# Super-step 0 of a delta-rule attention kernel in another order, with unused products in TensorE's waits

## The chip, the cores and the metric

The kernel runs on one core of one Trainium2 chip. The metric is device time in microseconds (us), from one launch to its end; smaller is better.

The engines are named as in the profile: PE is TensorE (matmul) and PEld its weight loads, DVE is VectorE, ACT is ScalarE, POOL is GpSimd, SP is SyncE, which here only issues DMAs. Each engine has a queue of its own and works it off in order; engines wait for each other through semaphores. TensorE writes to PSUM alone; ScalarE and VectorE copy from there to SBUF.

## The reference

Three layers follow each other. The first is a delta rule over 768 steps, for 4 batches of 8 heads of 48 dimensions; the other two are dense, on 3072 tokens.

```python
k_n = k / (np.linalg.norm(k, axis=-1, keepdims=True) + 1e-06)
for t in range(S):
    kt, vt, bt = (k_n[:, :, t], v[:, :, t], beta[:, :, t, None])
    y[:, :, t] = np.einsum('bhd,bhde->bhe', q[:, :, t], state)
    v_old = np.einsum('bhde,bhd->bhe', state, kt)
    state = state + bt[:, :, :, None] * np.einsum('bhd,bhe->bhde', kt, vt - v_old)
x = y.transpose(0, 2, 1, 3).reshape(B * S, H * D)        # 3072 x 384
h = np.maximum(x @ w_in, 0.0)                            # 384 -> 2048
x = h * h @ w_out                                        # 2048 -> 384
g = x @ w_gate                                           # 384 -> 1536
out = (g * (1.0 / (1.0 + np.exp(-g))) * (x @ w_val)) @ w_out2
```

## The kernel before, in words

**Super-steps.** The sequence is cut into six super-steps J of 128 steps, each into two chunks c of 64, and the 32 pairs of batch and head into two halves p of 16. Within a chunk the recurrence is solved in closed form: G = K K^T of the chunk, masked to its strict triangle and scaled by beta and the key norms, gives a matrix whose inverse (of 1 minus it) is needed. Then U = inverse times (V minus keys times state), Y = masked (K Q^T) times U plus the state's part, and the state gains K^T U. The dense layer 1 follows for the tokens of a super-step, in 16 slices m of 128 hidden features; layer 2 follows at the end for all.

**What stands at the start.** Super-steps 1 to 5 run their attention in the shadow of the dense layers of the step before. Super-step 0 has nothing to hide behind, so its order is written out by hand (lines 1154 to 1269), and for every engine alone: the manual schedule makes each engine's queue follow the order of the program's text. The line that calls a stage is `run(("name", ...))`; what a stage does is in the functions of the same name:
- `gram0` (line 437): G of a chunk on TensorE, into PSUM. `gd` (450) copies its four 32x32 diagonal blocks to DG, half p=0 on ScalarE, half p=1 on VectorE; `go` (461) copies an off-diagonal block, negated, to NT on ScalarE, two copies a call.
- `din` (499): VectorE transposes DG into T (a matrix per partition), copies the diagonal out (the squared norms), ScalarE takes their root, VectorE multiplies T by the mask BM (line 504), refines the root (`root`, line 377, eight operations on 32 columns) and multiplies T by beta (506).
- `inv0` (624): the inverse of the 16x16 blocks in T, on VectorE. `dout` and `nrows` transpose back, into ND and NDT. `d1` and `d2` (669, 687) merge 16x16 blocks to 32x32 on TensorE; `t11` transposes on VectorE; `dcopy` (521) copies the diagonal blocks from ND to NT, two copies on ScalarE and two on VectorE; `m1` and `m2` (710, 723) merge to 64x64, and their results are copied by ScalarE (p=0) and VectorE (p=1).
- `u` (753): U on TensorE, scaled by beta on VectorE (764). `y` (814, line 829): Y on TensorE, copied to x0, the input of the dense layer. `ku` (774) is the state's gain.
- `amm`, `acopy`, `asel`: K Q^T of a chunk on TensorE, copied by ScalarE, masked by GpSimd (595).
- `mcopy`, `mmask`, `mbeta`, `mout`, `tload`: G of super-step 1, copied by ScalarE, masked by GpSimd (482), scaled by VectorE (486), stored to DRAM by SP's queue (549) and read back as T, in which GpSimd runs the long inverse `inv` (600) of super-step 1.

**Conversion of weights.** The weights of layer 1 come in pieces (pc, kd) of 256 features, kd=0 of w_in and kd=1 of w_out, each as 64-bit words, and are turned into 32-bit floats: first an Abs on ScalarE (line 157, at `begin`), then three steps on VectorE (162, 164, 169). `conv(n)` does n of the steps, `ahead()` and `far(n)` begin the next piece or the next n. The Abs writes a buffer f, of which there is one while `held` is set, and two that alternate (by `turn`) afterwards. Slice m of the dense layer needs piece (m//2, 0) for its first product (line 952) and (m//2, 1) for its second (1031).

**The planner.** From line 1281 on, the dense slices of super-step 0 run with stages put between them at due times (`first`, in units of slices); a `slot` runs what is due and then as many conversion steps as a rate allows.

**Buffers.** PSUM has three buffers of tag "a", two of "h", three of "t". At the start half p=0 of most products goes to "a" and half p=1 to "t".

Of the kernel before, what the change touches and what calls it, by code (L numbers as in the profile page):

```python
# [8 lines left out]
F32 = mybir.dt.float32  # L9
# [3 lines left out]
ALU = mybir.AluOpType  # L13
# [8 lines left out]
def delta_attention_moe_moe2_kernel(  # L22
# [37 lines left out]
    nc = tc.nc  # L60
# [20 lines left out]
    ps_a = ctx.enter_context(tc.tile_pool(name="ps_a", bufs=3, space=bass.MemoryType.PSUM))  # L81
    ps_h = ctx.enter_context(tc.tile_pool(name="ps_h", bufs=2, space=bass.MemoryType.PSUM))
# [7 lines left out]
    ap = att.__enter__()  # L90
# [17 lines left out]
    ND, NDT, DG, BM = (t[:, 0:1024].rearrange("p (x t) -> p x t", t=32) for t in (own_w, own_v, own_h, own_l))  # L108
    ident = own_l[:, 1024:1152]
    TD = [t[:, 1024:1536].rearrange("p (u h t) -> p u h t", u=2, h=8) for t in (own_w, own_v)]  # L110
    KB = {}
    T = ap.tile([128, 32, 32], F32, name="T")
# [25 lines left out]
    turn = [0]  # L138
    held = [1]

    class Piece:
# [18 lines left out]
        def run(self):  # L160
            f, fi = self.f, self.f.bitcast(I32)
            nc.vector.tensor_scalar(out=fi, in0=fi, scalar1=3, scalar2=None, op0=ALU.logical_shift_left)  # L162
            yield
            nc.vector.scalar_tensor_tensor(  # L164
                out=self.d[:, 1], in0=self.d[:, 1], scalar=-0x80000000, in1=fi,
                op0=ALU.bitwise_and, op1=ALU.bitwise_or,
            )
            yield
            nc.vector.scalar_tensor_tensor(  # L169
                out=self.d[:, 1], in0=self.d[:, 0], scalar=29, in1=self.d[:, 1],  # L170
                op0=ALU.logical_shift_right, op1=ALU.bitwise_or,
            )
            yield
# [42 lines left out]
    begun = {}  # L216
# [3 lines left out]
    def load_w1(pc, kd, eng=nc.sync):  # L220
        if (pc, kd) == FIRST:
            raw = xp.tile([128, 2 * PIECE], I32, tag="xh", name="raw")
        else:
            raw = wp.tile([128, 2 * PIECE], I32, tag="w", name="raw")
        load_piece((w_in, w_out)[kd], pc, kd == 1, raw, eng)
        loaded[pc, kd] = raw
        landing[pc, kd] = 0 if startup else clock[0] + LAND + (eng is nc.sync)
# [24 lines left out]
    def ahead():  # L252

        if conv1 and landed(conv1[0]):
            begin(conv1[0])

    def far(n):

        for job in conv1[0:n]:
            if landed(job):  # L260
                begin(job)

    def landed(job):

        return job in loaded and clock[0] >= landing[job]
# [54 lines left out]
    startup = [True]  # L320
# [178 lines left out]
    def d_in():  # L499

        nc.vector.transpose(out=T, in_=DG.rearrange("s x t -> s t x"))
        nc.vector.tensor_copy(SS_, T.rearrange("p a b -> p (a b)")[:, 0:1024:33])
        nc.scalar.activation(out=A_, in_=SS_, func=ACTF.Sqrt)
        nc.vector.tensor_tensor(T, T, BM, op=ALU.mult)
        root(SS_, A_, B_, NT_, bT)
        nc.vector.tensor_tensor(T, T, bT.unsqueeze(1).to_broadcast([128, 32, 32]), op=ALU.mult)

# [302 lines left out]
    x0 = []  # L810
# [3 lines left out]
    def y0(c, p):  # L814

        if c == 0:
            pys = [
                (ps_t if g else ps_a).tile([128, KD, 64], F32, tag="t" if g else "a", name="ps_y") for g in range(2)
            ]
            rows = [slice(64 * g, 64 * g + 64) for g in range(2)]  # L820
        else:
            py = bank(p, [128, KD, 2, 64], "ps_y")
            pys = [py[:, :, g] for g in range(2)]
            rows = [slice(0, 112), slice(0, 128)]

        def product(quarter, g, h, w0, start, stop):

            q0, r = 32 * (quarter % 4), rows[g]
            nc.tensor.matmul(
                pys[g][q0:q0 + 32, quarter // 4], RSF[p][r, g, 64 * h + w0:64 * h + w0 + 32], AQ[c][r, p, g, h],  # L830
                start=start, stop=stop,
            )

        for i in range(4):
            for g in range(2):
                product(3 * i, g, 2 * i, 0, True, True)
                product(3 * i + 1, g, 2 * i, 32, True, False)
                product(3 * i + 2, g, 2 * i + 1, 16, True, True)
                product(3 * i + 1, g, 2 * i + 1, -16, False, True)
        if not x0:  # L840
            x0.append(xp.tile([128, KD, TOK], F32, tag="xl", name="x0"))
        t0 = c * HT + p * 128
        for y, t1, n in [(pys[0], t0, 64), (pys[1], t0 + 64, 64)] if c == 0 else [
            (py.rearrange("q k g t -> q k (g t)"), t0, 128)
        ]:
            ts = slice(t1, t1 + n)
            (copy2 if startup and t1 % 128 else copy)(x0[0][:, :, ts], y)

    def fetch_x(J, c0, n_):
        xr = ap.tile([128, KD, HT], F32, tag="xf", bufs=2, name="xr")  # L850
# [294 lines left out]
    def run_all(names):  # L1145
        for n in names:
            run(n)
# [3 lines left out]
            load_w1(pc, 0), load_w1(pc, 1)  # L1151


    pad = ap.tile([32, 16], F32, name="pad")
    nc.vector.memset(pad, 0.0)
    lead = ps_h.tile([128, 8, 64], F32, tag="h", name="ps_lead")
    for _ in range(15):
        nc.tensor.matmul(lead[0:16, 0, 0:16], pad, pad, start=True, stop=True)
    nc.vector.memset(TMP[:, 0:1], 1.0)
    nc.scalar.activation(out=TMP[:, 1:2], in_=TMP[:, 0:1], func=ACTF.Sqrt)  # L1160
    order = ctx.enter_context(ExitStack())
    order.enter_context(
        tc.manual_schedule(engines={mybir.EngineType.DVE, mybir.EngineType.Pool, mybir.EngineType.Activation})
    )

    def conv(n):

        conv_to(converted() + n)

    P2 = range(2)  # L1170
    mark = ap.tile([128, 1], F32, name="mark")

    def stage(w, J, c):
        run_all((w, J, c, p) for p in P2)

    def merge16(w, c):
        run_all((w, c, p) for p in P2)
# [19 lines left out]
    run(("v", 0, 0))  # L1197
    run(("v", 0, 1))
    load_w1(1, 0)
    nc.gpsimd.memset(mask, 0.0)  # L1200
    for b0 in (0, 64):
        nc.gpsimd.affine_select(
# [6 lines left out]
    run(("brows",))  # L1209
    for c in P2:  # L1210
        run_all(("gd", c, p) for p in P2)
    run(("din",))
    run_all(("go", c, p) for c in P2 for p in P2)
    run_all(("gram0", 1, c) for c in P2)
    run(("sums", 1, 0))
    run_all(("amm", 0, c) for c in P2)
    stage("mcopy", 1, 0)
    run(("sq", 1, 1, 0))
    stage("mcopy", 1, 1)
# [17 lines left out]
    ahead()  # L1237
    merge16("d2", 0)
    run(("t11", 0, 0))
    conv(1)  # L1240
    load_w1(0, 1, nc.scalar)
    run(("m1", 0, 0))
    run(("dcopy", 0))
    load_w1(1, 1, nc.scalar)
    load_w1(2, 0, nc.scalar)
    nc.gpsimd.tensor_copy(mark, NT[0][1][:, 0, 0:1])
    run(("m2", 0, 0))
    conv(2)
    load_w1(2, 1, nc.scalar)
    run(("asel", 0))  # L1250
    run(("asel", 1))
    run(("u", 0, 0))
    stage("mbeta", 1, 0)
    stage("mout", 1, 0)
    run(("y", 0, 0, 0))
    ahead()
    run(("y", 0, 0, 1))
    stage("mbeta", 1, 1)
    stage("mout", 1, 1)
    conv(3)  # L1260
    ahead()
    held.clear()
    run(("tload", 1, 0))
    run(("tload", 1, 1))
    run(("v", 1, 0))
# [15 lines left out]
    if True:  # L1281
# [7 lines left out]
        for J in range(NJ):  # L1289
            seq += [(J, c0, HT, m) for c0 in (0, HT) for m in range(HMS[J])]  # L1290
            seq += [(J, 0, TOK, m) for m in range(HMS[J], NM1)]
        first = {
            0: [("d1", 1, 0), ("d1", 1, 1), ("abs", 2), ("ku", 0, 0)],
            0.5: [("abs", 2), ("d2", 1, 0), ("d2", 1, 1), ("loadw", 3, 0, nc.scalar)],
            1: [("ks", 0, 1), ("t11", 0, 1), ("dcopy", 1), ("loadw", 3, 1, nc.scalar)],
            1.5: [("loadw", 4, 0, nc.scalar)],
            2: [("m1", 0, 1), ("loadw", 4, 1, nc.scalar)],
# [55 lines left out]

        moe1_h(*seq[0])
        moe1_low()
        far(1 + len(begun))
        for n, it in enumerate(seq):
            J, c0, n_, m = it
            if n and J and not seq[n - 1][0]:
# [111 lines left out]
```

## Time and profile before

| | us |
|---|---|
| median of 3 runs | 1034.11 (1033.69 to 1034.76) |
| time of the profiled execution | 1035.7 |
| span of the profiled execution | 1034.0 |
| PE busy | 995.0 |
| DVE busy | 588.2 |
| ACT busy | 401.2 |
| POOL busy | 251.2 |

The span is the time from the program's first instruction to its last, in one profiled execution. A row of the profile tells of a group of instructions: the line of the kernel, the engine, the operation, what it writes and reads (out<-in, by the program's names), partitions x elements, and how many (x). In a timeline the first two numbers are the start and the time in us from the first instruction's start to the last's end; in brackets stands the idle time of the engine before it, and what ended it. "issue" is time for which the profile shows nothing that was waited for. POOL's times are rough, and matmuls overlap in their pipeline, so that the mean of a run of them is the time of the run over their count.

### The profile page before, as it was taken

The page shows a single profiled execution, that of the slowest core. Times are in us where ns is not written, and L with a number is a line of the kernel's source. Part 1 is how long each engine was busy: PE and PEld are TensorE (multiplying, and loading weights), DVE is VectorE, ACT ScalarE, POOL GpSimd, SP SyncE. Part 2 cuts the span into 40 slices and gives each one's busy share as a digit, 9 for nine tenths or more (in the row PEclk, how much of TensorE's full clock was granted, in tenths as well). Part 3 has the DMA queues.
Part 4 walks back from the last instruction along what each step waited for, and adds up shares of the span by engine and source line. Part 5 has one row for each costly group of instructions (what it writes and reads, how often), then busy time and mean ns, then how long its engine had stood idle before and what let it go on. Part 6 is the DMA issues. An engine that isn't in the chain of part 4 may idle for free.

```text
span 1034.0 us, 24233 instructions
## 1 busy us (share of the span) xinstructions
PE 995.0 (96%) x10508; PEld 813.4 (79%) x10508; DVE 588.2 (57%) x951; ACT 401.2 (39%) x752; POOL 251.2 (24%) x368
## 2 busy tenths in 40 slices
PE   5688999999999999999999999999999999999998
PEld 4577657888788888888888778888888888888886
DVE  7889977866776575554269973343433433433333
ACT  6375465432532443343368841221312221311212
POOL 3669588038218407700000000000000000000000
PEclk9999999999999999999999999999999999999999
DMA  9488434362354424211146620100100100100000
GB/s 260 154 256 222 102 95 130 74 142 68 106 134 96 105 58 94 71 50 33 32 167 198 223 84 1 61 1 1 61 1 1 61 0 1 61 1 1 31 1 30
DMA packets 118393, 84.49 MB, mean 82 GB/s; under 512 B 91664, under 2 KB 95888, under 8 KB 118288
## 3 DMA queue, kind: packets, MB, share of 16 engines
q1 hardware_dynamic: 113712, 69.98, 25.2%
q10 hardware_dynamic: 3520, 8.26, 2.4%
q0 software_dynamic: 1056, 4.72, 1.2%
q8 instruction: 82, 1.34, 0.6%
q14 instruction: 23, 0.19, 0.1%
HBM read 61.70 MB, written 21.23 MB: 80 GB/s over the span
## 4 chain that ended last, share of the span: by engine, by line
PE 59%; issue 11%; DVE 11%; DMA 8%; POOL 8%; ACT 2%; SPq 1%; ACTq 0%; DVEq 0%; POOLq 0%
PE ps_o L1127 14%; PE ps_g L1102 13%; PE ps_v L1102 13%; PE ps_h L983 6%; PE ps_y L1031 6%; POOL T L619 4%; POOL TMP L612 4%; DMA x2raw<-y_scr 1%; DVE raw L164 1%; DMA raw<-in_moe_w_out_dram 1%; DMA raw<-in_moe_w_val_dram 1%; DVE raw L169 1%; DMA AQ<-in_q_dram 1%; DMA m_scr<-M 1%; DVE f L162 1%
## 5 line engine op out<-in xcount | busy, mean ns | idle before, releaser
L983 PE MATMUL ps_h<-xh,w 128*128 128x512 f32 (+1 forms) x540 | 168.2, 372 | 0.1
L1102 PE MATMUL ps_g<-x2h,w 128*128 128x512 f32 x432 | 144.8, 390 | 0.0
L1102 PE MATMUL ps_v<-x2h,w 128*128 128x512 f32 x432 | 144.8, 390 | 0.0
L1106 DVE SCALAR_TENSOR_TENSOR th<-th,ps_g 128x512 f32<-128x512 f32 x72 | 49.5, 687 | 167.5 <-ACT th L1105 167.2
L1031 PE MATMUL ps_y<-hh,w 128*128 128x512 f32 (+1 forms) x552 | 138.1, 383 | 2.4 <-DVE ye L1046 1.8
L612 POOL TENSOR_TENSOR TMP<-T 128x30 f32<-128x30 f32 (+9 forms) x150 | 95.3, 635 | 141.8 <-DMA T<-m_scr 96.4
L986 ACT ACTIVATE r<-ps_h 128x512 f32<-128x512 f32 (+1 forms) x90 | 49.3, 548 | 172.6 <-PE ps_h L983 162.5
L1031 PEld LDWEIGHTS ps_y<-hh,w 128*128 128x128 f32 x552 | 98.1, 188 | 22.9 <-PE ps_h L983 2.3
L983 PEld LDWEIGHTS ps_h<-xh,w 128*128 128x128 f32 x540 | 98.6, 189 | 17.9 <-ACT xh L861 0.3
L1127 PE MATMUL ps_o<-ph,w 128*128 128x512 f32 x432 | 111.6, 390 | 0.0
L1105 ACT ACTIVATE th<-ps_g 128x512 f32<-128x512 f32 x72 | 43.0, 597 | 175.1 <-PE ps_g L1102 175.1
L619 POOL TENSOR_TENSOR T<-T,TMP 128x30 f32<-128x30 f32 (+9 forms) x150 | 99.5, 663 | 11.4
L983 PE MATMUL ps_h<-xl,w 128*128 128x512 f32 (+1 forms) x270 | 99.5, 368 | 0.4 <-DVE xl L862 0.4
L1109 ACT ACTIVATE ph<-th 128x512 fp32r<-128x512 f32 x72 | 45.5, 632 | 132.8 <-DVE th L1107 132.8
L1102 PEld LDWEIGHTS ps_g<-x2h,w 128*128 128x128 f32 x432 | 81.1, 188 | 16.8
L1127 PEld LDWEIGHTS ps_o<-ph,w 128*128 128x128 f32 x432 | 81.1, 188 | 16.8
L1102 PEld LDWEIGHTS ps_v<-x2h,w 128*128 128x128 f32 x432 | 81.1, 188 | 16.8
L1004 DVE TENSOR_TENSOR r<-r 128x512 f32<-128x512 f32 (+1 forms) x73 | 48.7, 667 | 70.9 <-ACT hh L987 70.4
L1102 PE MATMUL ps_g<-x2l,w 128*128 128x512 f32 x216 | 84.2, 390 | 0.0
L1102 PE MATMUL ps_v<-x2l,w 128*128 128x512 f32 x216 | 84.1, 390 | 0.0
L1031 PE MATMUL ps_y<-hl,w 128*128 128x512 f32 (+1 forms) x276 | 75.1, 377 | 1.5 <-DVE hl L1005 1.4
L1005 DVE TENSOR_TENSOR hl<-r,hh 128x512 fp32r<-128x512 f32 (+1 forms) x96 | 66.2, 690 | 18.2 <-ACT r L1002 8.1
(162 smaller groups left out, 1475.3 us busy)
## 6 DMA issues: line engine op xcount, KB each, us to landing
raw<-in_moe_w_out_dram SPq DMA_DIRECT2D x8, 768.0 KB, 6.1
KT<-in_kt_dram SPq DMA_DIRECT2D x12, 448.0 KB, 6.8
m_scr<-M SPq DMA_DIRECT2D x20, 256.0 KB, 2.6
KB<-in_kn_dram SPq DMA_DIRECT2D x12, 384.0 KB, 6.5
AQ<-in_q_dram SPq DMA_DIRECT2D x24, 192.0 KB, 5.5
V<-in_v_dram SPq DMA_DIRECT2D x12, 384.0 KB, 4.4
raw<-in_moe_w_out_dram ACTq DMA_DIRECT2D x6, 768.0 KB, 6.9
raw<-in_moe_w_gate_dram SPq DMA_DIRECT2D x6, 768.0 KB, 4.4
```

The source lines that it names most:

```text
L612: eng.tensor_tensor(tmp[:, r0:r1], t_[:, r0:r1, kk:kk + 1].to_broadcast([n, r1 - r0, w]), t_[:, kk:kk + 1, kk + 1:].to_broadcast([n, r1 - ...
L619: eng.tensor_tensor(t_[:, r0:r1, kk + 1:], t_[:, r0:r1, kk + 1:], tmp[:, r0:r1], op=ALU.add)
L983: nc.tensor.matmul(ps, w_[:, kk], x_[:, kk, cols], start=n == 0, stop=n == 3 * KD - 1)
L986: nc.scalar.activation(out=r, in_=ps, func=ACTF.Relu)
L1004: nc.vector.tensor_tensor(r, r, r, op=ALU.mult)
L1005: nc.vector.tensor_tensor(hl, r, hh.bitcast(F32), op=ALU.subtract)
L1031: nc.tensor.matmul(acc[f], w_[:, fs], h_, start=first, stop=m == NM1 - 1 and n == len(terms) - 1)
L1102: nc.tensor.matmul(ps, w_[:, kk], x_[:, kk], start=n == 0, stop=n == 3 * KD - 1)
L1105: nc.scalar.activation(out=th, in_=gp, func=ACTF.Tanh, scale=0.5)
L1106: nc.vector.scalar_tensor_tensor(out=th, in0=th, scalar=1.0, in1=gp, op0=ALU.add, op1=ALU.mult)
L1109: nc.scalar.activation(out=hh, in_=th, func=ACTF.Copy)
L1127: nc.tensor.matmul(o_acc[J][f], w_[:, fs], h_, start=m == 0 and n == 0, stop=m == NM2 - 1 and n == 2)
```

## The change

Five things are done, all in super-step 0 and in the first slots behind it.

- In `din`, the product of T with the mask BM goes from VectorE to GpSimd.
- Stages are called in another order: three of the four `go` ahead of `din`; `dcopy` and the one `conv` step behind it ahead of `m1`; the other two steps of the first piece, which stood ahead of `u`, behind it, with one half of `y` between them; `mbeta` and `mout` of chunk 0 of super-step 1 behind those of chunk 1 and behind the three steps of piece (0, 1). Piece (0, 1) is loaded by SP's queue behind (1, 0), not by ScalarE's ahead of `m1`.
- The last copy of Y for chunk 0 goes from VectorE to ScalarE.
- In place of 15 small products on a tile of zeros, TensorE starts with 6 of 160 columns on part of T, and products whose result nobody reads (`spin`) stand at five places of its queue: 9 of 192 columns ahead of `d1`, and one of 256 columns ahead of `m1`, of `m2`, of `u` and of `y`. They use the first keys as data and a PSUM buffer of tag "a".
- Pieces are begun later: `far(1)` behind the first dense product, where `held` now ends, and one piece in the first slot's list, behind `ku`, in place of two ahead of it; the list of the second slot has its two behind `d2`.

```diff
-        nc.vector.tensor_tensor(T, T, BM, op=ALU.mult)
+        nc.gpsimd.tensor_tensor(T, T, BM, op=ALU.mult)
...
-            (copy2 if startup and t1 % 128 else copy)(x0[0][:, :, ts], y)
+            (copy2 if startup and t1 == 64 else copy)(x0[0][:, :, ts], y)
...
-    pad = ap.tile([32, 16], F32, name="pad")
-    nc.vector.memset(pad, 0.0)
-    lead = ps_h.tile([128, 8, 64], F32, tag="h", name="ps_lead")
-    for _ in range(15):
-        nc.tensor.matmul(lead[0:16, 0, 0:16], pad, pad, start=True, stop=True)
+    def turn_over(tile_, w, n, cols):
+
+        flat = w.rearrange("q a b c -> q (a b c)") if len(w.shape) == 4 else w.rearrange("q a b -> q (a b)")
+        for _ in range(n):
+            nc.tensor.matmul(
+                tile_.rearrange("q h t -> q (h t)")[:, 0:cols], flat[:, 0:128], flat[:, 0:cols], start=True, stop=True
+            )
+
+    nc.vector.memset(T[:, 0:5], 0.0)
+    turn_over(ps_h.tile([128, 8, 64], F32, tag="h", name="ps_lead"), T, 6, 160)
...
+    def spin(n, cols):
+
+        turn_over(ps_a.tile([128, 8, 64], F32, tag="a", name="ps_spin"), KB[0, 0], n, cols)
...
     load_w1(1, 0)
+    load_w1(0, 1)
...
+    run_all(("go", c, p) for c, p in ((0, 0), (0, 1), (1, 0)))
     run(("din",))
-    run_all(("go", c, p) for c in P2 for p in P2)
+    run(("go", 1, 1))
     run_all(("gram0", 1, c) for c in P2)
     run(("sums", 1, 0))
     run_all(("amm", 0, c) for c in P2)
+    spin(9, 192)
...
     run(("t11", 0, 0))
+    spin(1, 256)
+    run(("dcopy", 0))
     conv(1)
-    load_w1(0, 1, nc.scalar)
     run(("m1", 0, 0))
-    run(("dcopy", 0))
+    spin(1, 256)
...
     run(("m2", 0, 0))
-    conv(2)
+    spin(1, 256)
...
     run(("u", 0, 0))
-    stage("mbeta", 1, 0)
-    stage("mout", 1, 0)
+    spin(1, 256)
+    conv(1)
     run(("y", 0, 0, 0))
     ahead()
+    conv(1)
     run(("y", 0, 0, 1))
     stage("mbeta", 1, 1)
     stage("mout", 1, 1)
     conv(3)
-    ahead()
-    held.clear()
+    stage("mbeta", 1, 0)
+    stage("mout", 1, 0)
...
-            0: [("d1", 1, 0), ("d1", 1, 1), ("abs", 2), ("ku", 0, 0)],
-            0.5: [("abs", 2), ("d2", 1, 0), ("d2", 1, 1), ("loadw", 3, 0, nc.scalar)],
+            0: [("d1", 1, 0), ("d1", 1, 1), ("ku", 0, 0), ("abs", 1)],
+            0.5: [("d2", 1, 0), ("d2", 1, 1), ("abs", 2), ("loadw", 3, 0, nc.scalar)],
...
-        far(1 + len(begun))
+        far(1)
+        held.clear()
+        turn[0] = 0
```

## Rows read from the trace of the kernel before

**Rows 1.** The page: busy us (share of the span) and instructions of each engine
```profile
PE 995.0 (96%) x10508; PEld 813.4 (79%) x10508; DVE 588.2 (57%) x951; ACT 401.2 (39%) x752; POOL 251.2 (24%) x368
```

**Rows 2.** Busy time by stretch: PE, PEld, DVE, ACT, POOL, PEclk, DMA share, GB/s
```profile
24.64:28.39 3.75, 0.01 (x1) 0.03 (x1) 3.71 (x12) 3.68 (x7) 0.19 (x1) 1.00 0.12 42
...
60.00:91.50 31.50, 29.40 (x627) 24.80 (x626) 28.84 (x36) 18.13 (x36) 28.72 (x36) 1.00 0.93 265
...
95.10:98.50 3.40, 3.40 (x24) 2.69 (x14) 3.15 (x4) 2.94 (x6) 3.17 (x4) 0.50 1.12 280
98.50:131.00 32.50, 32.25 (x346) 21.09 (x344) 28.77 (x39) 16.51 (x29) 19.66 (x28) 1.00 0.40 89
```

**Rows 3.** TensorE's waits in the first 50 us: total us, times, longest
```profile
PE ps_g L430 <- DMA KT<-in_kt_dram: 6.7, 2, 3.4
...
PE ps_e L693 <- issue: 1.6, 1, 1.6
...
PE ps_y L829 <- issue: 1.1, 1, 1.1
```

**Rows 4.** Timeline of ScalarE and VectorE around the mask and the root
```profile
13.11 0.23 ACT L503 ACTIVATE TMP<-TMP 128x32 f32<-128x32 f32 x1 [2.63 <-DVE TMP L502]
13.11 1.22 DVE L504 TENSOR_TENSOR T<-T,own 128x1024 f32<-128x1024 f32 x1
13.36 3.11 ACT L466 ACTIVATE NT<-ps_g 32x256 f32<-32x256 f32 x8
14.26 0.17 DVE L379 TENSOR_SCALAR TMP<-TMP 128x32 f32<-128x32 f32 x1
...
16.35 1.22 DVE L506 TENSOR_TENSOR T<-T,TMP 128x1024 f32<-128x1024 f32 x1
```

**Rows 5.** Timeline from 28 us: GpSimd's product, and a root beside it
```profile
28.44 1.91 POOL L519 TENSOR_TENSOR NT<-NT,bB 128x1024 f32<-128x1024 f32 x1 [2.76 <-issue]
...
30.02 0.37 DVE L379 TENSOR_SCALAR NS<-NS 128x32 f32<-128x32 f32 x1 [0.57 <-ACT NS L371]
```

**Rows 6.** Timeline of GpSimd and VectorE, from 33 to 51 us
```profile
33.38 5.34 POOL L482 TENSOR_TENSOR M<-M,mask 128x512 f32<-128x512 f32 x4
...
36.60 0.88 DVE L702 COPY tq<-ps_m 32x256 f32<-32x256 f32 x2 [1.45 <-PE ps_m L715]
...
37.51 1.95 DVE L529 COPY NT<-ND 32x512 f32<-32x512 f32 x2
...
39.48 0.86 DVE L702 COPY NT<-ps_x 32x256 f32<-32x256 f32 x2
...
43.14 2.31 DVE L764 TENSOR_TENSOR RS<-ps_u,bB 64x384 f32<-64x384 f32 x4
...
50.77 0.96 DVE L164 SCALAR_TENSOR_TENSOR raw<-raw,f 128x768 int32<-128x768 int32 x1
```

**Rows 7.** Timeline of TensorE, from 28 to 62 us
```profile
28.39 1.90 PE L675 MATMUL ps_d<-NDT,ND 16*32 16x16 f32 x128 [3.75 <-DVE nB L510]
...
39.60 2.87 PE L758 MATMUL ps_u<-V,NT 64*64 64x48 f32 x62 [0.17 <-DVE NT L529]
43.82 3.08 PE L829 MATMUL ps_y<-AQ,RS 64*32 64x64 f32 x122 [1.36 <-DVE RS L764]
...
49.17 5.28 PE L952 MATMUL ps_h<-x,raw 128*128 128x256 f32 x12 [0.50 <-issue]
54.38 1.28 PE L675 MATMUL ps_d<-NDT,ND 16*32 16x16 f32 x128
...
60.79 1.57 PE L952 MATMUL ps_h<-x,raw 128*128 128x256 f32 x6
```

**Rows 8.** Timeline of ScalarE and VectorE, from 57 to 60 us
```profile
57.22 1.99 ACT L788 ACTIVATE RS<-ps_s 48x384 f32<-48x384 f32 x4 [0.71 <-PE ps_s L779]
...
60.01 0.56 DVE L162 TENSOR_SCALAR f<-f 128x768 int32<-128x768 int32 x1 [2.14 <-ACT f L157]
```

**Rows 9.** TensorE's waits from 76 to 135 us
```profile
PE ps_a L563 <- DMA AQ<-in_q_dram: 2.1, 2, 1.7
```

## The prediction, made before the change was run

> **What bounds the kernel now.** I read the page's busy shares first: TensorE is busy for 995.0 of 1034.0 us [rows 1], so no edit that stays clear of TensorE can gain, and what is to be had lies in its idle time and in work at the lower clock. The view of its waits puts most of the idle time into the first 50 us: 6.7 us until the first keys land, 3.75 us until the diagonal blocks are inverted (ps_d waits for VectorE) [rows 7], and waits in the middle of a block of small products that no semaphore ends, named "issue" (1.6 us in ps_e, 1.1 us in ps_y) [rows 3]. The timeline of that stretch shows the chain: VectorE's work on T, d1, d2, the transposes, m1, m2, U, Y, and at 49.17 us the first products of the dense layer [rows 4, 6, 7]. From there on TensorE has work to the end, so a microsecond won at 49 us is kept only if later waits don't return it.
>
> The clock column of the page says 1.00 throughout the start, yet the durations do not: twelve dense matmuls of 256 columns took 5.28 us from 49.17 on, 440 ns each, and six of the same shape took 1.57 us at 60.79, 262 ns each with the tail [rows 7]. Since the engine has two levels, 1.2 and 2.4 GHz, I take everything before about 54 us to run at the lower one.
>
> **The change, part by part.**
>
> *The lead.* Fifteen products of 16 columns become six of 160. One call is two matmuls here (twelve for two groups of three calls [rows 7]), so 12 x 440 x 160/256 = 3.3 us, inside the 3.4 us wait for the keys [rows 3]. Cost nothing; with that cover gone, about 0.5 us.
>
> *The mask on GpSimd.* VectorE gives up one operation of 1.22 us at 13.11 [rows 4]; the sum in between, from 14.26 to 16.35, stays (2.09 us). GpSimd starts at about 13.05 (it needs the diagonal read first) and takes 1.91 us, as its product of the same size does [rows 5]: done at 14.96. If both ran side by side, the root would run 13.4 to 15.5, a gain of 0.85 us. But while that GpSimd product ran (to 30.35), VectorE's first root operation took 0.37 us and ended at 30.39; alone it takes 0.17 [rows 4, 5]. So I let the first root operation end at 15.0, and the other 1.92 us follow: 16.9, a loss of 0.6 us. The Trainium skill, page "SBUF — State Buffer", section "SBUF: two separate sides", says that VectorE and GpSimd share a port pair that one of them holds for a whole instruction while the other fully blocks. The row agrees (it ended 0.04 us behind GpSimd's); by that rule the sum is +0.6 us, without it -0.85 us.
>
> *Off-diagonal copies ahead of the root.* Six of the eight copies (3.11/8 = 0.39 us each [rows 4]) now stand before ScalarE's Sqrt: 2.3 us, into 2.63 us in which it waited [rows 4]. Nothing on the path; without that cover 2.3 us.
>
> *Piece (0,1) on SP's queue* stands behind everything that the start needs, and in front of M's stores, which come 20 us later. Its 768 KB fall on a stretch in which the DMA engines are 12% busy [rows 2]. ScalarE loses one issue of it. Nothing.
>
> *Nine unused products of 192 columns* stand in TensorE's queue ahead of d1. 18 matmuls of 330 ns (440 x 192/256) are 5.9 us at the lower level, 3.5 us at the higher by 262 ns. They start at 24.6 and the wait that they fill is 3.75 us. Behind them queue d1, and behind d1 everything. If the clock rises during them, as it did during the dense products behind 49.17, they end at about 30.0; d1 starts 1.6 us late (bounds: 0.6, which is the mask's, to 2.2). The mask's 0.6 is covered by this. At the higher level d1 needs 0.6 us less (its 128 matmuls took 1.90 us at 28.39 and the same count for the second chunk 1.28 at 54.38 [rows 7]) and d2, by the same ratio, some 0.4; the "issue" wait I leave at its 1.6. So d2 ends 0.6 us later than now.
>
> *Diagonal blocks and one conversion step ahead of m1.* VectorE's queue now has, behind the transposes, two copies of ND, then L162, then the copies that m1's second half and m2 wait for. Now the latter start at 36.60, after 1.45 us of idle time [rows 6], so L162 ended at 35.15 and the transposes 0.5 before it: 34.7, with the 0.6 late start 35.3. That idle time would hold 2 x 0.44 + 0.56 us (copies as L702's, and L162) [rows 6, 8]. But GpSimd runs its four mask products there (33.38 to 38.72, 1.33 us each), and L529's two copies, which free would need 0.88 us, took 1.95 from 37.51 on: the first, I read, ended only when GpSimd's last did [rows 6]. Taking turns, each of the three waits for one such product: 36.8, 38.2, 39.7. m1's copies then end at 40.6 instead of 37.5 (unhindered: 38.1). After them m2 needs 0.6 us and its copies no longer stand behind ND's: they end at 42.1 instead of 40.3. I take the hindered value, since L529's row is this very operation beside this very neighbour; free, it is 2.3 us less.
>
> *Conversion behind U.* U's last 60 matmuls ran from 40.4, when m2's copies were done [rows 6], to 42.47 [rows 7]. At the higher level they take 1.1 us, from 42.1 to 43.3. Now two conversion steps stand ahead of U's scaling, which starts at 43.14, 0.7 us behind U; afterwards it starts at 43.3 and ends at 45.6 (2.31 us [rows 6]), about as now. The conversion now follows: two steps of 0.96 [rows 6], a copy between them of 0.4, 0.3 us for GpSimd: 48.2. M's products with beta are put behind it. TensorE's Y is done by then, including its "issue" wait, and the last copy is ScalarE's. The dense products start at 48.2 instead of 49.17.
>
> *The single unused products* lie in waits for VectorE or ScalarE; 0.5 us each at the higher level. Nothing, unless their PSUM buffer is late.
>
> *The dense products* at the higher level: 12 x 262 = 3.1 us instead of 5.28, ending 3.1 us earlier than now.
>
> *Conversions begun later.* Piece (1,1)'s first step on ScalarE now stands behind ku's copies (1.99 us, to 59.2 today [rows 8]), so VectorE idles before (1,1) instead of before (2,0), where it idles 2.14 us now [rows 8]. With TensorE 3.1 us early, VectorE is about 2.6 early at 64 us.
>
> *What is late next.* From 60 to 91.5 us VectorE is busy for 28.84 of 31.5 us and the DMA engines for 93% [rows 2]. Moving TensorE ahead does not move the bytes: ps_a waits 2.1 us for AQ at 91.5 [rows 9], and the clock then stands at its lower level (0.50) for 3.4 us [rows 2], which costs half of that. I let 0.6 of the 2.6 be returned there: -2.0 us.
>
> The sum is made against the profiled execution: 1035.7 us, span 1034.0. The median of the runs, 1034.11, is 1.6 below it. 1035.7 - 2.0 = 1033.7 under the profiler, and 1034.1 - 2.0 = 1032.1 us as a median. A measurement of this kernel can tell 0.2%, 2.07 us, from no change, so the forecast stands on that bound.
>
> **The rivals.**
>
> *No hindrance.* VectorE slips its copies between GpSimd's products, and the path gains the 2.3 us. For it: the copies are short and GpSimd's gaps exist. Against it: L529's row. AQ takes part of it: -4.2, 1029.9 us.
>
> *The clock falls back before U.* From d1 to Y there are small products and waits only; in the rows the level fell after the 2.1 us wait at 91.5 [rows 2, 9]. Then U needs 2.07 us again, its scaling ends at 46.6, the dense products run from 49.0 for 5.28 us: 54.3 against 54.45. Same as now, 1034.1 us.
>
> *VectorE starved (slower).* Its place is ScalarE's order behind the first dense products. If the unused products run out at the lower level, d1 starts 2.2 us late and the dense products end at 55.1; ku's copies then end at 59.9, (1,1) starts at 60.8 and (2,0) at 63.3 instead of 60.01 [rows 8], 3.3 us late. Idle time left on VectorE up to 131 us is 2.7 + 3.7 us [rows 2], most of it waits; a third of the delay is made good, 2.3 us are left: 1036.4. It decides once (2,0)'s L162 starts after about 62 us.
>
> **How the numbers follow.** Forecast (1032.1) 0.42, no hindrance 0.18, clock falling back 0.20, starved 0.20. Faster by over 0.2% (below 1032.04): half of the forecast, 0.21, and 0.17 of the second: 0.38. Slower by over 0.2% (above 1036.2): 0.17 of the last and 0.02 of the third: 0.19. Within: 0.43. The range takes in the unhindered case with the mask's gain hidden, and the starved one: 1029.7 to 1036.6; the forecast's own is 1030.9 to 1033.3.
>
> **What would show it.** The dense matmuls of line 952 near 250 ns and their start before 48.5; the mask's product on GpSimd near 1.9 us with L379 ending right behind it; L529's copies over 1 us each; (2,0)'s L162 before 60; ps_a's wait for AQ longer than 2.1 us. I am wrong if d1 starts before 28.4, if the twelve dense matmuls still take 5 us, or if the wait for AQ is gone.

## The result, and the profile after

The changed kernel takes 1044.81 us in the median of five runs (1044.03 to 1045.94), the kernel before 1034.3 beside it: a ratio of 1.0111, 95% interval [1.0098, 1.0125]. It is slower, by 10.5 us between the medians and by 11.5 us (1.11% of 1034.3) by the ratio, and outside the predicted range. The experiments below are compared by their ratios, so parts of the loss are given as parts of 11.5 us. The profiled execution has a span of 1044.0 us.

The first 51 us came out nearly as forecast. TensorE's timeline of the changed kernel (start, duration, engine, line, operation, count, idle time before it):

```profile
28.98 1.27 PE L675 MATMUL ps_d<-NDT,ND 16*32 16x16 f32 x128 [1.16 <-DVE nB L510]
...
41.56 1.96 PE L758 MATMUL ps_u<-V,NT 64*64 64x48 f32 x64
...
48.31 2.87 PE L952 MATMUL ps_h<-x,raw 128*128 128x256 f32 x12 [0.81 <-ACT x L698]
51.10 1.30 PE L675 MATMUL ps_d<-NDT,ND 16*32 16x16 f32 x128
```

The twelve dense matmuls take 2.87 us instead of 5.28 and are followed by the second chunk's d1 at 51.10 instead of 54.38 [rows 7]: TensorE is 3.3 us early. Seventy microseconds later it is 9.9 us late. The same view from 115 us on, and VectorE's:

```profile
124.25 0.32 PE L743 MATMUL ps_k<-RS,KT 48*64 48x48 f32 x4
131.56 1.95 PE L743 MATMUL ps_k<-RS,KT 48*64 48x48 f32 x60 [7.00 <-DVE M L538]
```
```profile
130.82 0.69 DVE L538 SCALAR_TENSOR_TENSOR M<-ps_g,mask 128x512 f32<-128x512 f32 x1 [12.59 <-DMA m_scr<-M]
```

TensorE may write ps_k only when VectorE has read ps_g (L538), and VectorE had no buffer for M until M's earlier stores were out. In the kernel before that read stands at 120.16 and ps_k at 121.67, and TensorE does not wait for it. Following the wait back, from engine to engine, first SyncE's queue and then GpSimd's first operation of the inverse:

```profile
48.62 4.67 SPq L549 DMA_DIRECT2D m_scr<-M  x4
57.48 7.31 SPq L554 DMA_DIRECT2D T<-m_scr  x4
...
121.25 0.35 SPq L646 DMA_DIRECT2D n_scr<-T  x1
128.03 6.74 SPq L549 DMA_DIRECT2D m_scr<-M  x4
```
```profile
75.21 0.25 POOL L612 TENSOR_TENSOR TMP<-T 128x30 f32<-128x30 f32 x1 [29.22 <-DMA T<-m_scr]
```

M's stores of super-step 2 (128.03, before 117.40) stand in SP's queue behind the store of the inverse (121.25, before 109.51). The inverse started at 75.21 instead of 60.04, because T's loads landed at 64.9, 70.2, 72.0 and 75.0 us instead of 55.6 to 59.9. What lay beside these loads, ScalarE's queue:

```profile
57.33 0.39 ACTq L136 DMA_DIRECT2D raw<-in_moe_w_in_dram  x1
...
59.14 0.37 ACTq L136 DMA_DIRECT2D raw<-in_moe_w_out_dram  x1
...
59.55 0.52 ACTq L136 DMA_DIRECT2D raw<-in_moe_w_in_dram  x1
```

Three weight pieces of 768 KB are issued between 57.33 and 59.55, among T's loads (57.48 to 61.76). In the kernel before they were issued at 60.92, 62.82 and 63.23, when T had landed. In the DMA view from 57 to 64 us T's loads take 12.5 us in the median from issue to landing:

```profile
raw<-in_moe_w_in_dram ACTq DMA_DIRECT2D x2, 768.0 KB, 9.2
raw<-in_moe_w_out_dram ACTq DMA_DIRECT2D x1, 768.0 KB, 8.5
T<-m_scr SPq DMA_DIRECT2D x4, 128.0 KB, 12.5
```

From 52 to 64 us in the kernel before, the four took 3.6 us. Beside the wait, TensorE's other losses:

```profile
PE ps_k L743 <- DVE M L538: 7.0, 1, 7.0
PE ps_a L563 <- DMA AQ<-in_q_dram: 2.5, 1, 2.5
PE ps_u L758 <- issue: 2.4, 1, 2.4
```

and the stretches at the lower level behind these waits (columns as in [rows 2]; the seventh is the granted clock):

```profile
74.30:81.10 6.80, 6.42 (x37) 4.78 (x38) 4.46 (x7) 2.79 (x5) 5.03 (x12) 0.50 1.05 376
...
94.70:101.60 6.90, 6.70 (x74) 5.49 (x75) 3.44 (x5) 3.97 (x7) 6.27 (x9) 0.51 0.98 275
128.90:135.70 6.80, 4.14 (x63) 2.96 (x64) 4.77 (x7) 0.00 (x0) 0.00 (x1) 0.50 0.63 139
149.40:152.80 3.40, 3.40 (x9) 0.87 (x11) 2.38 (x3) 2.07 (x5) 3.09 (x5) 0.50 0.00 0
```

The kernel before had one such stretch between 54 and 200 us, 3.4 us long [rows 2].

The wait at ps_k is only a part of the loss: TensorE comes to ps_k at 124.25, already 2.6 us later than before, although it was 3.3 us early at 51. T's slow loads hold SP's queue in another way too. V's load behind them is issued at 64.89 instead of 55.47 us, and the weight piece behind that at 70.25 instead of 56.65; ScalarE's next Abs waits 4.63 us until T has landed, and VectorE waits for the Abs:

```profile
64.89 5.30 SPq L313 DMA_DIRECT2D V<-in_v_dram  x1
```
```profile
75.54 0.90 ACT L157 ACTIVATE f<-raw 128x768 f32<-128x768 f32 x1 [4.63 <-DMA T<-m_scr]
...
76.48 0.56 DVE L162 TENSOR_SCALAR f<-f 128x768 int32<-128x768 int32 x1 [4.26 <-ACT f L157]
```

The first two stretches above are 13.7 us at half the clock where the kernel before has 3.4. If TensorE lost half of the difference, that is some 5 us, an estimate. That these stretches come of the crowded loads is argued from their order in time; no run separates them from the rest.

### The profile page after: what moved, and what is told of

It is laid out like the page before. It is cut to its first block, busy times and chain, and to the rows that moved or that the text cites. A ratio compares the mean times of both kernels' runs of the same rounds, so it can differ in the third digit from the quotient of the medians.

```text
span 1044.0 us, 24243 instructions
## 1 busy us (share of the span) xinstructions
PE 1006.4 (96%) x10516; PEld 820.6 (79%) x10516; DVE 582.2 (56%) x949; ACT 401.3 (38%) x753; POOL 246.3 (24%) x369
## 4 chain that ended last, share of the span: by engine, by line
PE 61%; POOL 11%; issue 10%; DVE 8%; DMA 7%; ACT 1%; SPq 1%; DVEq 0%; POOLq 0%; ACTq 0%
PE ps_o L1127 14%; PE ps_g L1102 14%; PE ps_v L1102 14%; PE ps_y L1031 7%; PE ps_h L983 7%; POOL T L619 5%; POOL TMP L612 5%; DMA T<-m_scr 2%; DMA raw<-in_moe_w_val_dram 1%; DMA m_scr<-M 1%; PE ps_y L795 1%; DVE raw L164 1%; PE ps_u L758 1%; PE ps_g L430 1%; PE ps_a L563 1%
## 5 line engine op out<-in xcount | busy, mean ns | idle before, releaser
L1106 DVE SCALAR_TENSOR_TENSOR th<-th,ps_g 128x512 f32<-128x512 f32 x72 | 49.5, 687 | 167.1 <-ACT th L1105 166.6
L612 POOL TENSOR_TENSOR TMP<-T 128x30 f32<-128x30 f32 (+9 forms) x150 | 91.5, 610 | 158.8 <-DMA T<-m_scr 74.3
```

What stands on the lines that cost most here:

```text
L612: eng.tensor_tensor(tmp[:, r0:r1], t_[:, r0:r1, kk:kk + 1].to_broadcast([n, r1 - r0, w]), t_[:, kk:kk + 1, kk + 1:].to_broadcast([n, r1 - ...
L1106: nc.vector.scalar_tensor_tensor(out=th, in0=th, scalar=1.0, in1=gp, op0=ALU.add, op1=ALU.mult)
```

## Experiments

All ratios are to the kernel before, run on the same chip between the others (medians of 1031.9 to 1033.4 us there).

My theory: M's chunk 0, moved behind chunk 1 and three conversion steps, is stored late; TensorE, 3 us early, brings ScalarE's weight loads forward; T's loads meet them; GpSimd's inverse is late and holds SP's queue. The rivals: the clock's falls and the waits in the middle of a block, brought by the unused products, do it whatever M does; or the late stores alone do it.

**M's chunk 0 back where it was (e1).**

```diff
     run(("u", 0, 0))
+    stage("mbeta", 1, 0)
+    stage("mout", 1, 0)
     spin(1, 256)
...
     conv(3)
-    stage("mbeta", 1, 0)
-    stage("mout", 1, 0)
```

> M's chunk 0 (products with beta, stores) back where the kernel before has it, right behind U; all else as in the changed kernel. Theory (the late stores of M let the loads of T run into ScalarE's weight pieces; GpSimd's inverse then ends 12 us late and holds SP's queue): chunk 0's stores at about 49 us instead of 52.3, T's loads issued at about 53 and landed by 61, the inverse starting near 61 and ended by 110, the wait for ps_k near nothing; the dense products start about 2 us later because VectorE's last copy of Y stands behind 2.6 us of products: 1033 us (1030 to 1036). Rival (the loss is the clock's falling back and the waits for code in the middle of a block, whatever M does): 1042 us or more, with the inverse early.

1034.04 us, ratio 1.0015 [1.0005, 1.0025]. 9.9 of the 11.5 us go with this one edit, so the theory's place is right and the first rival falls as a cause of the loss: all unused products are still there. (The 1.5 us that stay are of the size of e9's and e12's below, with the unused products and without them.) T's loads are issued from 51.84 and the inverse starts at 59.83. But one forecast missed: the wait at ps_k is not near nothing.

```profile
118.33 0.32 PE L743 MATMUL ps_k<-RS,KT 48*64 48x48 f32 x4
121.27 1.94 PE L743 MATMUL ps_k<-RS,KT 48*64 48x48 f32 x60 [2.62 <-DVE M L538]
```

TensorE arrives 3.3 us earlier than in the trace of the kernel before and goes on at 121.27, where it stood there (121.67).

**Late stores alone, in the kernel before (e2); with earlier weights (e16); the change with later weights (e3).** e2 moves M's chunk 0 behind `conv(3)` in the kernel before. e16 is e2 with

```diff
-            0: [... ("abs", 2), ("ku", 0, 0)],
+            0: [... ("abs", 2), ("ku", 0, 0), ("loadw", 3, 0, nc.scalar), ("loadw", 3, 1, nc.scalar)],
```

and ("loadw", 4, 0) moved from 1.5 to 0.5. e3 is the changed kernel with the pieces (3,0) to (4,1) about one slice later each.

> The kernel before with M's chunk 0 put behind chunk 1 and three conversion steps, and nothing else. Theory, if the order of M alone does it: chunk 0's stores at about 53 us, T's loads landing near 72 beside the weights, the wait for ps_k some 7 us: 1041 to 1045 us. If it takes both halves (the stores late and the weight loads 3.6 us early with TensorE): T's loads still land before the weights, by 63 us, inside the slack of 12 us: 1034 to 1035 us. Rival (clock and code waits of the unused products): 1034 us too, and e1 then stays slow.

> e2 (the kernel before with M's chunk 0 behind the conversion) with the loads of pieces (3,0), (3,1) and (4,0) one product earlier on ScalarE's queue; no unused products, TensorE no earlier. Theory (it takes M's late stores and the weights on the DMA engines together, and nothing else of the change): T's loads, issued from 56.5, land after 66, the inverse's store is issued after 114, ps_k waits 3 us or more: ratio 1.006 to 1.010. Rival (it takes the early TensorE or the unused products): e2's ratio of 1.0036 within 0.002.

> The changed kernel with the loads of pieces (3,0), (3,1), (4,0) and (4,1) on ScalarE's queue one product later each; M as changed. Theory (the weights on the DMA engines hold T's loads): T's loads, issued from 57.5 on, land by 64 and the inverse starts near 64 instead of 75; ps_k waits under 2 us: 1034 to 1038 us, if the later weights don't starve VectorE (in that case 1038 to 1042 with new waits of VectorE for DMA). If lateness of M's stores alone does it, without the weights: T's loads still land after 70 and the time stays at 1044.

e2: 1034.2 us, 1.0036 [1.0017, 1.0055]. The median is the case that takes both halves; by the ratio the late stores alone already cost 3.7 us. Its runs spread from 1033.0 to 1042.3, and the profiled one, the quickest, doesn't show why. e16: 1044.95 us, 1.0127 [1.0110, 1.0144]. e3: 1039.41 us, 1.0064 [1.0049, 1.0079]. GpSimd's first operation of the inverse in e2, e16 and e3:

```profile
62.73 0.25 POOL L612 TENSOR_TENSOR TMP<-T 128x30 f32<-128x30 f32 x1 [16.68 <-DMA T<-m_scr]
```
```profile
69.56 0.25 POOL L612 TENSOR_TENSOR TMP<-T 128x30 f32<-128x30 f32 x1 [23.67 <-DMA T<-m_scr]
```
```profile
66.85 0.64 POOL L612 TENSOR_TENSOR TMP<-T 128x30 f32<-128x30 f32 x1 [21.19 <-DMA T<-m_scr]
```

Late stores delay the inverse by 2.7 us (60.04 in the kernel before; 3.5 us against the 59.27 of e15 below); with the weights beside T's loads it is 9.5 us late, and TensorE waits as in the changed kernel:

```profile
130.60 1.95 PE L743 MATMUL ps_k<-RS,KT 48*64 48x48 f32 x60 [7.15 <-DVE M L538]
```

e16 has no unused product, no mask on GpSimd and no early TensorE, and is as slow as the change, beyond my 1.010. So these two things together are shown to make a loss as large as the change's. That the early weights alone would not is not shown; in e1 the first of these pieces is issued at 60.76, when T has landed. e3 got less than half back, 4.9 of 11.5 us, 1.4 us above the range for weights that starve nobody: T's last load landed at 66.7, not by 64, and ps_k still waits 5.7 us. That the later weights cost something of their own there isn't excluded: between 55 and 125 us VectorE waits 4.0 us in all for ScalarE's Abs, against 2.1 in the kernel before.

**The link through SP's queue (e4).** The store of the inverse and its loads behind M's four stores of super-step 2:

```diff
-            10.5: [("nout", 1)],
-            11: [... ("nback", 1, 0), ("nback", 1, 1), ("gram", 2, 0)],
-            13: [("gram", 2, 1), ("tload", 2, 0)],
+            11: [... ("gram", 2, 0)],
+            13: [("gram", 2, 1), ("nout", 1), ("nback", 1, 0), ("nback", 1, 1), ("tload", 2, 0)],
```

> The changed kernel with the store of the inverse and the loads of it put behind M's four stores of super-step 2 in SP's queue. Theory (the late inverse does its harm by holding SP's in-order queue, so M's stores, M's buffers, VectorE and ps_k): VectorE's wait of 12.6 us for a buffer of M and TensorE's 7.0 us for ps_k at 124 us go, though the inverse still ends near 121; some comes back where m1 of super-step 1 waits for the inverse: 1036 to 1040 us. Rival (the wait at ps_k is of other origin): it stays, 1044 us.

1037.79 us, 1.0056 [1.0034, 1.0077]. The inverse is as late as before (stored at 123.34), VectorE's read stands at 117.69 without a wait, and TensorE doesn't wait at ps_k either:

```profile
123.22 1.15 PE L743 MATMUL ps_k<-RS,KT 48*64 48x48 f32 x64
```

5.7 of the 11.5 us were thus SP's order, as expected. The other half stays, and with it the late arrival: TensorE comes to ps_k at 123.22 here, at 123.13 in e16, at 119.93 in e3 and at 118.33 in e1. e4 has 10.2 us at the lower level ahead of it (76.0 to 79.4 and 93.1 to 99.9 us).

**Why e1 is not faster than the kernel before (e5, e6).** e5 is e1 with e4's edit, e6 the kernel before with it.

> e1 (M's chunk 0 back behind U) with, besides, the inverse's store and its loads put behind M's four stores of super-step 2 in SP's queue. Theory (with M repaired TensorE is still 3 us early at 118 us, but the end of GpSimd's inverse, through SP's queue and VectorE's buffer of M, stands where it stood, so TensorE waits 2.6 us at ps_k and then runs 6.8 us at the lower level): both go, 2.6 + 3.4 us below e1's 1034: 1028 us (1027 to 1031). Rival (the 3 us are stopped again at the next thing that needs the inverse, m1 of super-step 1): 1032 us or more, with a wait of over 2 us at ps_m or ps_k of super-step 1.

> The kernel before with that same edit of SP's order alone. There TensorE reaches ps_k less than 1 us behind VectorE's read of ps_g, so nothing waits: 1031 to 1032.5 us, ratio 0.999 to 1.001, if the edit is worth something only to a TensorE that is early. Rival (the edit is a gain of its own): 1029 us or less.

Both missed: e5 1.0032 [1.0012, 1.0051], e6 1.0027 [1.0014, 1.0040]. The wait at ps_k is gone in e5 (119.49), but T's next loads now stand behind eight loads of the inverse, the next inverse ends 3 us later, and GpSimd's scaling of V behind it stops VectorE and then TensorE. VectorE's and TensorE's rows of e5 near 181 us:

```profile
181.76 1.69 DVE L751 TENSOR_TENSOR V<-V,ps_k 128x384 f32<-128x384 f32 x3 [2.86 <-POOL V L318]
```
```profile
PE ps_h L983 <- DVE xl L862: 3.3, 1, 3.3
```

So GpSimd's chain (T's loads, inverse, its store, M's stores, T's next loads, next inverse, V) is a second chain beside TensorE's, and TensorE meets it at 120 and, in e5, again at 181 us.

**The inverse made earlier (e9, e11), the unused products without the rest (e12, e14, e7), the kernel before again (e15).** e9 is the change, e11 the kernel before, with M's chunk 0 ahead of U's scaling, in VectorE's wait for U; e11 has its two conversion steps behind it:

```diff
+    stage("mbeta", 1, 0)
+    stage("mout", 1, 0)
     run(("u", 0, 0))
```

> The changed kernel with M's chunk 0 multiplied and stored ahead of U's scaling, in VectorE's wait of 2.2 us for U; chunk 1 stays where the change has it. Theory (two things pace the kernel from 51 to 184 us: TensorE, and GpSimd's chain from the loads of T over the inverse to the next inverse; the change made the first 3 us early and the second late, e1 left the second where it was): T's last load lands at about 57 us instead of 59.9, the inverse ends at about 106.5, n_scr is stored 3 us earlier than in the kernel before, the waits at ps_k (118) and behind V's scaling (181) don't grow, and TensorE keeps 2 to 3 us: ratio 0.997 to 0.998. Rival (the gain is given back wherever it is, to the weights): ratio 1.000 to 1.002 with an early inverse, and waits for DMA or AQ longer than in e1.

> The kernel before with its chunk 0 of M and its two conversion steps changing places around U (M ahead of U's scaling, the conversion behind it), nothing else: the chain of the inverse early, TensorE as before. Theory: the inverse ends 2 us or more earlier, VectorE's wait for a buffer of M (1.43 us) goes, TensorE isn't early and gains nothing: ratio 0.998 to 1.001. Rival (GpSimd's chain alone sets the pace): ratio 0.997 or less.

> The kernel before, unchanged, for a trace of it beside the others: ratio 1.000; the wait at ps_k near nothing, the inverse stored at 109 to 111 us.

e9: 1.0016 [1.0005, 1.0026]; the gain that I expected did not come. The inverse was stored at 108.30, 1.2 us and not 3 us earlier than in the kernel before, and TensorE no longer waits at ps_k (119.15). e10 is e9 with chunk 1 of M moved up too, right behind U; it was expected within 0.1% of e9, or 1 us or more below it if only the inverse counted. It came to 1.0015 [1.0006, 1.0025]: the inverse was stored at 106.83, and the time is e9's. e11: 0.9992 [0.9982, 1.0002], as expected, though VectorE's wait for a buffer of M stayed (1.25 us). e15: 1.0001 [0.9988, 1.0015], and its trace corrects my reading of the first one:

```profile
117.70 0.32 PE L743 MATMUL ps_k<-RS,KT 48*64 48x48 f32 x4
120.11 1.14 PE L743 MATMUL ps_k<-RS,KT 48*64 48x48 f32 x60 [2.10 <-DVE M L538]
```

In this execution the kernel before itself comes to ps_k 4.0 us earlier than in the one I predicted from, and waits there for M. In that one TensorE had just been held 2.1 us by AQ [rows 9] and slowed behind it [rows 2], so it came as M was ready. In the kernel before too, then, a lead at 51 us would have met GpSimd's chain at 120.

The unused products: e12 is e9, e7 is e5, each without the thirteen in the waits; e14 is e11 with them and the new lead.

> e9 without the thirteen unused products in the waits. If the unused products pay: the twelve dense matmuls take 5 us again, TensorE is 2 to 3 us later at 54 us, and with the inverse out of the way this stays: 2 us above e9. Rival (they are worth nothing): within 1 us of e9.

> e5 without the thirteen unused products in the waits (the six at the very start stay). If they pay by the clock: d1, d2 and the dense products at the lower level, dense products 5.3 us instead of 2.9, TensorE some 3 us later at 60 us, and 3 us of it kept: 1031 us. Rival (the clock is at its lower level from 33 to 46 us all the same, and what TensorE gains by 60 us is given back later): the same as e5 within 0.1%.

> e11 (the kernel before with M's chunk 0 ahead of U's scaling, ratio 0.999) with the unused products of the change and nothing else of it: six of 160 columns at the start, nine and four single ones in the waits. Theory (the clock's gain is real and is kept when the inverse isn't in its way): the twelve dense matmuls take about 2.9 us, TensorE is 2 us ahead of e11 at 60 us, ratio 0.997 to 0.998. Rival (what TensorE is ahead by goes into waits for the weights and into stretches at the lower level behind those waits): ratio 0.999 to 1.001.

e12: 1.0020 [1.0010, 1.0030] against e9's 1.0016. e7: 1.0052 [1.0033, 1.0071] against e5's 1.0032 [1.0012, 1.0051]. e14: 0.9998 [0.9989, 1.0008] against e11's 0.9992. In no pair do the intervals part: what the unused products are worth (0.04%, 0.2%, -0.06%) can't be told from nothing. But only the first pair tests the prediction's gain: there the twelve dense matmuls take 5.20 us without them (e12) and 2.86 with them (e9). In e5 they take 4.52 with them and 5.41 without (e7), and in e14, against its expectation, 5.46 with them and 4.47 without (e11): there the level was not up when the dense products came.

**The mask (e8) and the order of beginnings (e13).** e8 is e5 with the mask on VectorE, e13 is e9 with the kernel before's order of beginnings.

> e5 with the mask of T back on VectorE. By the prediction's step the root's end comes 0.5 to 0.6 us earlier (1.22 us of mask on VectorE against a first root operation that lasted 2.18 us beside GpSimd), d1 0.5 us earlier, the rest follows: 0.5 us below e5. Rival (the move frees VectorE): 0.5 to 1 us above e5.

> e9 (the change with M's chunk 0 ahead of U's scaling) with the order in which conversions are begun on ScalarE put back to the kernel before's. If the later beginnings cost: VectorE's wait of 2 us or more for ScalarE behind piece (1,1) goes, 1 us below e9, ratio 1.000 to 1.001. If they are worth nothing: e9's ratio of 1.0016 within 0.001.

e8: 1.0034 [1.0017, 1.0051], no difference from e5. From the diagonal's read to the product with the root VectorE needs 3.54 us in e8 (12.31 to 15.85), as before, and 4.73 in e5 (12.17 to 16.90): the move costs 1.2 us there. Yet d1 starts at 28.86 and 28.95: in e8 it stands right behind the nine unused products. e13: 1.0012 [1.0002, 1.0022]: nothing.

**M's first stores past the inverse, T's next loads not delayed (e17, e18).** e17 is e9, e18 the kernel before, with

```diff
-            10.5: [("nout", 1)],
-            11: [... ("nback", 1, 0), ("nback", 1, 1), ("gram", 2, 0)],
+            11: [... ("gram", 2, 0), ("nout", 1), ("nback", 1, 0), ("nback", 1, 1)],
```

> e9 (the change with M's chunk 0 ahead of U's scaling) with the inverse's store and its loads put between M's stores of chunk 0 and of chunk 1 in SP's queue, not behind both as in e5. If ps_k's wait for GpSimd's chain is what every version runs into at 120 us: M's first stores are issued at 108 to 111 instead of 115, the inverse's loads at most 1 us later, no wait of VectorE for a buffer of M, ps_k's wait gone, the next inverse no later than in e9: ratio 0.996 to 0.998. Rival (the time goes again to m1 of super-step 1 or to V's scaling at 181, as in e5): 1.000 or more.

> The kernel before with that same edit alone. TensorE reaches ps_k at 118 us there and waits 2.1 us (e15), then runs 3.4 us at the lower level: without both 2 to 3.5 us less, ratio 0.997 to 0.998. If e17 is below it by 1 us or more, TensorE's early start is worth something once this wait is gone; if the two agree, the unused products are worth nothing even then.

e17: 0.9992 [0.9981, 1.0003]. e18: 0.9986 [0.9977, 0.9996], 1032.16 us against 1033.41: the only version whose interval lies below both kernels, by 0.14%, less than the 0.2 to 0.3% I expected. e17 is not below it, though its twelve dense matmuls take 2.87 us. The wait is gone:

```profile
118.26 0.68 DVE L538 SCALAR_TENSOR_TENSOR M<-ps_g,mask 128x512 f32<-128x512 f32 x1
...
119.92 1.39 DVE L538 SCALAR_TENSOR_TENSOR M<-ps_g,mask 64x512 f32<-64x512 f32 x2
```
```profile
119.83 1.15 PE L743 MATMUL ps_k<-RS,KT 48*64 48x48 f32 x64
```

TensorE is no earlier there than e15's 120.11. Start of the second, 16th, 17th and 33rd ReLU of the dense layer, in us:

```
                      2nd     16th    17th    33rd
e15 (before again)    54.23  115.23  127.85  219.00
changed kernel        51.54  121.78  139.30  231.38
e1                    53.75  116.37  129.00  220.03
e9                    52.28  118.37  126.73  219.64
e14                   53.50  118.15  125.70  217.97
e18                   54.61  119.19  126.95  218.00
e16                   55.04  120.66  138.34  229.49
```

What stands at 54 us doesn't order the last column. From the 17th on each keeps its distance but for stretches at the lower level (changed kernel 149.4 to 152.8 us, e9 136.4 to 139.8, e14 135.0 to 138.4).

Open: where e9 and e17 lose their lead of 2 us between 55 and 115 us, where VectorE is busy for 28.84 of 31.5 us [rows 2] and the leads of one version differ by 2 us and more from those of the next without an order that I could read.

## Why the prediction was wrong

*The step that failed* is "M's products with beta are put behind it", which I priced at nothing, and "What is late next" with it, where I followed VectorE, the bytes and AQ only. M's order feeds another chain: store, T's loads, an inverse of 46 to 51 us on GpSimd, SP's queue, M's buffers, ps_k. The trace of the kernel before told that this chain had no slack. VectorE's row there:

```profile
120.16 0.69 DVE L538 SCALAR_TENSOR_TENSOR M<-ps_g,mask 128x512 f32<-128x512 f32 x1 [1.43 <-DMA m_scr<-M]
```

It had itself waited for M's store, and ended 0.8 us before ps_k. That M's last store would go some 2.5 us later could be read from the new order too (three conversion steps of 0.56 + 0.96 + 0.96 us [rows 6, 8]; it went 2.6 later, 52.91 for 50.33). What made 2.6 into 15 is the meeting with the weights, and for that one more thought was needed: a TensorE that is early lets ScalarE issue its loads early. e2, e16 and e3 show both parts.

*The sum's term of -2.0 us* was wrong too: the sum kept 2.0 of the 3.1 us by which the dense products end earlier. In e9, with M early, they end at 51.89 instead of 54.45 and TensorE does not wait for GpSimd at 120 us; the kernel is no faster (1.0016), nor than e12 (1.0020), where they end at 53.75. TensorE comes to ps_k at 119.15, later than e15's 117.70, and where the lead went stays open. One place where it would have stopped was there to be read in a second trace: I read "TensorE has work to the end" from one execution in which the wait at 120 us was hidden by another.

*What was right.* The dense matmuls near 250 ns (2.87 us / 12 = 239 ns) and their start before 48.5 (48.31); (2,0)'s L162 at 58.87, before 60, so VectorE was not starved there; AQ's wait 2.5, longer than 2.1; L529's copies 2.51 us for two. d1 at 28.98 instead of 30.0: the nine unused products took 5 us, ending at 27.8, ahead of d1's inputs. m1's copies ended at 39.4 and not at 40.6. The clock did fall back before U, as that rival had it: U took 1.96 us, at the lower level, and the level rose again at 47 us, in time for the dense products.

*The mask* was mis-sized: +0.6 us forecast, 1.2 measured between the diagonal's read and the product with the root. GpSimd took 2.35 us instead of the 1.91 of [rows 5], and L379 with it:

```profile
12.51 2.35 POOL L504 TENSOR_TENSOR T<-T,own 128x1024 f32<-128x1024 f32 x1 [1.61 <-DVE TMP L502]
```
```profile
12.71 2.18 DVE L379 TENSOR_SCALAR TMP<-TMP 128x32 f32<-128x32 f32 x1 [0.36 <-ACT TMP L503]
```

It ended 0.03 us behind GpSimd's, an operation that alone takes 0.17 us [rows 4]. This is what the Trainium skill's page "SBUF — State Buffer", section "SBUF: two separate sides", says of the two engines' shared port: one holds it for a whole instruction. The trace agrees. The page says it of some of VectorE's operations only, those in a two-port mode or with two inputs from SBUF, and the prediction left this out. In a later root beside another product of GpSimd the reciprocal was not held (0.35 us, as alone), and the product with two inputs was (1.02 us, alone 0.19), to 0.05 us behind GpSimd's end:

```profile
30.89 1.47 POOL L318 TENSOR_TENSOR V<-V,nB 128x768 f32<-128x768 f32 x1
31.00 0.35 DVE L380 RECIPROCAL NS<-NS 128x32 f32<-128x32 f32 x1
31.39 1.02 DVE L381 TENSOR_TENSOR NS<-NS 128x32 f32<-128x32 f32 x1
```

On the kernel's time e8 shows no effect of the mask.

## What to carry to other kernels

Before an order is changed, follow every moved instruction's DMA to its last reader, through each queue that is in order, even where the engine that issues it is idle: here two products of 0.64 us each, moved by 6 us, cost some 10 us once the weights came early too. A wait that is near nothing in one trace may be two chains that meet; a second trace of the same kernel (e15) shows which of them arrives first and what a lead is worth. And an engine that gets ahead also issues its loads earlier: ask what they will meet.

## What the runs showed of the hardware that was not expected

Here small loads suffered out of proportion beside large ones: T's four loads of 128 KB took 3.6 us in the median to land in the kernel before (DMA share 0.90 from 52 to 60 us), and 12.5 us beside three pieces of 768 KB on another engine's queue (1.01 from 57.3 to 75.1). The pieces of w_in themselves went only from 7.1 to 9.2. In e16 the first of T's loads, issued 0.36 us ahead of the first weight piece, landed after 2.8 us; the second, 0.03 us behind it, after 8.1.

From its first operation to its store the same inverse took 46.0 us in the changed kernel (75.21 to 121.25), where VectorE was busy for 34.0 of them, 49.5 in the kernel before (60.04 to 109.51, VectorE busy for 44.6) and 50.6 in e1 (59.83 to 110.41, 48.3). The wait of the mask's root, seen from the other side, fits that, but no run isolates it.
